# Batch 2's first dense layer by seven half-size products

## The chip, the cores and the metric

The kernel runs on one core of a Trainium2 chip. The metric is the device time of one execution in microseconds. PE below is the tensor engine (PEld its weight loads, which overlap its products), DVE the vector engine, ACT the scalar engine, POOL the GpSimd engine, SP the engine that only issues transfers here.

## The reference

Attention with a sliding window and sink tokens, and behind it a dense layer, a squared ReLU and a second dense layer:

```python
# q, k, v: (4 batches, 8 heads, 768 tokens, 64), float32; n_sink = 4, window = 128
scores = q @ k.T / sqrt(64)
keep   = (key < 4) | (0 <= query - key < 128)
a      = softmax(where(keep, scores, -1e9))
x      = (a @ v), heads side by side           # (3072 tokens, 512)
h      = x @ w_in                              # w_in  (512, 2048)
g      = maximum(h, 0) ** 2
out    = g @ w_out                             # w_out (2048, 512), float32
```

## The kernel before

The kernel works in bf16 with float32 sums. It takes one batch of 768 tokens after another, in three steps of 256 tokens (`s`), and lays the attention of batch b+1 between the dense layers of batch b, so that PE always has something to multiply. Every piece of work is an operation of a small planner (`op(...)`), with the engines it may run on and what it comes after. Which operation is issued when, on which engine, and in which room of a pool, isn't decided at run time: the string `ORDER` lists the operations by number, with a letter where the engine was chosen (d, a, g for DVE, ACT, POOL) and a `+0` or `+1` for the pool. Each engine then works through its list strictly in that order, and waits where an input or a room isn't ready.

**Attention.** K and Q of batches 2 and 3 are loaded by POOL (lines 393, 403 for V) and turned by transposing transfers on SP's queue (line 449). PE makes scores (line 602), ACT the exponentials (623), POOL or DVE the masks (213, 632, 635), PE the values (671), DVE the division (687, 688), and SP's queue turns the result into `xT` (702).

**First dense layer, plain form** (`layer1`, line 752): for 2 or 4 blocks of 128 hidden features, four products each over the 512 inputs, with 512 or 256 tokens as the moving columns, into a PSUM room of pool `den`. Then a ReLU (DVE 765 or ACT 763) and a square (DVE 774 or ACT 772) into `gT_sb`. Batches 0, 1 and 2 use it.

**First dense layer, fast form** (`layer1_fast` and `quad`, line 872): batch 3 alone uses it (`FAST = (3,)`). It halves the hidden features, the inputs and the tokens, and makes the 2 by 2 block product with seven half-size products instead of eight (Strassen). A quad is one group of blocks: seven products of 8 matmuls with 128 tokens, or of 4 matmuls with 256 tokens. It holds two PSUM banks from its first product to its last reading, in pool `den` or `att`; `den` and `att` have two rooms each, and `att` also serves the scores and the values. Around the products stand sums of tokens (line 830; for a single step of 256 tokens after a spreading copy `xd` on ACT), a copy of the first product (ACT or DVE, 187/189), two subtractions (DVE, 913), a ReLU for half of the result (ACT 928 or DVE 930), a sum with saturation for the other half (DVE, 940), and two squares (894, 896). Inside a quad these alternate with the products: the fifth product waits for the copy, the fourth and third for the subtractions, the sixth and seventh for the ReLU.

**Weight sums.** The fast form needs five sums of weight blocks of `w_in`. Each was one DVE operation of 2048 elements a partition (line 796). Three were written over `qkT_all[0]` (free once batch 2's attention is done), two into rooms of pool `qr`, which has five.

**Second dense layer**: the plain form for two thirds of batch 0 (961), and the same seven-product scheme (`layer2_fast`, line 1071) elsewhere, with its sums (1029), additions out of PSUM (1096, 1112, 1119) and copies.

Of the kernel before, what the change touches and what calls it, by code (L numbers as in the profile page):

```python
# [21 lines left out]
0 8 7 9 1 5 10 11 2 12 13 3 14 15 55d 57+0 16 19 59a 20 17 56d 21 18 61d 63+0 22 58 62d 65a 60d 64 6 67a 83+1 79 66a  # L22
68d 69+1 85 70 71d 103+0 84+0 105 73g 74d 72d 23 75+1 86 76 77d 91+0 78a 24 87+1 93 25 89 88 92+0 80 26 114+1 90 94
95+0 4 96 117 97 106g 99+1 98 104+0 107 100d 101 118g 81+1 102d 113+0 108d 156 115 127 82 116d 119+1 157a 121 27 28
120 109+0 111 29 30 31 32 33 158a 122 162 110 112 123+1 125 168 126a 124d 163d 171 169d 164d 165 172a 173d 159 166a
167a 128 131 130d 129d 177 160a 133a 132a 137 145 140 174 148 161d 178d 179d 136 144 289 290 146 149d 170d 147d 138
139d 134 141d 135 175d 34 208g 291 35 36 37 38 39 40 41 42 43 44 45 46 47 48 49 50 51 52 53 54 355 356 292 150 142
143 151 293 294 274 295 152 154 153d 296 297a 176a 298a 155d 186 275 187a 276 277 196+0 180 198a 183 181a 182a 184a
197 204+1 205 199d 188d 200+0 201 192+0 193 189 206a 207d 194d 203d 195d 190d 202a 219+0+0 191d 185d 357 358 359 220
222 278 279 212+0+1 213 215 300 209 301 280 281 373 385d 223 302 237+0+0 210+1 282 299 374 375 376 211 238 240 304  # L30
305 214 239d 306d 230+0+0 307 308 233 231 216 303 311 309d 310 217+0 221 224+0 312 315 234g 232g 313 218 360 314 225
235+0 283 316 241d 242+0 236 317a 284 243 361 362 363 364 365 366 367 368 369 370 371 226+1 228 251+0 229d 286a 227a
244+0 246 252d 253d 245a 285 247d 389 287d 248+1 390 392 340 249d 250d 256+0+0 341a 325 259 257 391 260d 393 326d
386 254+0 322 258g 382 255 342a 263+0+0 323a 261+1 334 262 324d 335d 264 266 265g 396 383 379 288 378 372 267d 331
397 399 398 327a 337 268+0 332d 377 380 384 381 269 319 338a 339d 270+0 271a 272 320d 400 273a 336a 333a 328 321d
329d 330d 456 394 401 352 343 437 353a 349 344a 402 395 530 560g 531 532 533 551 534 535 536 537 538 539 458 318 405
350a 457 351d 441 443d 439 438 345d 406 408 346 412 442 444 445 415 553 403 347d 413 447 409g 416g 428 348a 446a 549
554 548 407g 429 440 448 449 450 414d 451 460 387 354a 461 452 431 388 410 417 475 476 453 454a 479 411 432g 430g
480 463 481a 459 477 418 478 421 482 483 550 552 455 419 422 484a 424 555 404 465a 423g 425g 420 462a 485 433 486
487 490 464 434 488 426 672 489 466 427 467 468 471 580 540 541 542 543 544 545 491 492d 469 494 581 583 470 472  # L40
473d 503 670 495d 435 493 556 559 436 558 557 496a 564 500 565 567 504d 669 509 501d 566 587 510a 512 505a 588 590
568 561 673 511d 497 513d 571 515 574 671 498d 499a 569 572 506 502d 570 514d 516a 575 573 603 521 606 604 507d 522d
546 584g 591g 605g 547 527 576 562 577 518 517a 508a 528a 612 613 582d 631 632 633 519a 563 520a 589g 524 596 597
# [68 lines left out]
def kernel(  # L112
# [11 lines left out]
    nc = tc.nc  # L124
# [245 lines left out]
    def load_v(b, s, behind=None, yields=()):  # L370
# [8 lines left out]
        ops["cast", b, s] = o  # L379

    def load_natural(b, s, older_values):

        begun = [ops["layer1", b - 2, 0, 0], w_out_op[3]]
        for ti in (1, 0):
            if s == 0:
# [395 lines left out]
    def weight_sums_in(key, after):  # L781
# [4 lines left out]
        for n, (name, x, y, how) in enumerate(((1, A[0][0], A[1][1], ALU.add), (2, A[1][0], A[1][1], ALU.add),  # L786
# [4 lines left out]
            def run(e, n=n, name=name, x=x, y=y, how=how, slot=slot):  # L791
                if slot is None:
                    wi_sb[name] = spare[n]
                else:
                    wi_sb[name] = bank(slot, "wi", [128, 2, 2, 512], BF16)
# [473 lines left out]
```

## Time and profile before

| | |
|---|---|
| median of 3 runs | 213.5 us (213.03 to 213.55) |
| the profiled execution | 213.66 us, its span 211.9 us |
| PE busy | 204.0 us, 96% of the span |
| DVE busy | 167.8 us, 79%, 303 instructions |
| ACT busy | 112.9 us, 53%, 146 instructions |
| POOL busy | 97.9 us, 46% |
| granted PE clock | 1.00 |
| weight loads (PEld) busy | 165.1 us, 78% |

The 1.76 us between the profiled execution's time and its span lie before the first and after the last instruction. The mean duration of an instruction is longer than its distance to the next one: on PE the ends are modelled and overlap, and on DVE and ACT the groups add up to about 181 and 120 us, against 167.8 and 112.9 us busy, because one instruction begins before the one ahead has quite ended. So PE work is counted here by the pieces of the chain (start to start), and sums on DVE and ACT are scaled by 167.8/181 = 0.93 and 112.9/120 = 0.94.

### The profile page before, as it was taken

The numbers are of one execution on the slowest core, as the hardware profiler recorded it, in microseconds if no ns is written. First come the engines' busy times: TensorE is split into PE (matmuls) and PEld (weight loads), VectorE is DVE, ScalarE is ACT, GpSimd is POOL, SyncE is SP. The second block draws the span as 40 slices with busy tenths as digits, with TensorE's granted clock in tenths as the row PEclk, the third lists the DMA queues.
The fourth block names the chain that finished last, engine by engine and source line by source line (L and its number), as shares of the span: only waits on it lengthen the run. The fifth ranks groups of instructions, "written<-read, shape, count | busy, mean of one in ns | idle before, by whom it ended". The sixth has DMA issues, their size and how long they took to land.

```text
span 211.9 us, 5455 instructions
## 1 busy us (share of the span) xinstructions
PE 204.0 (96%) x2282; PEld 165.1 (78%) x2287; DVE 167.8 (79%) x303; ACT 112.9 (53%) x146; POOL 97.9 (46%) x139
## 2 busy tenths in 40 slices
PE   3999999999999999999999999999999999999993
PEld 3858997579569645589888964569899999998892
DVE  7487747795898847798776699997979989899963
ACT  2497277249652488567854234887931017976100
POOL 7989696598409965792851951216400000000000
PEclk9999999999999999999999999999999999999999
DMA  5999999999992999999933899304404504000205
GB/s 138 295 186 206 174 198 215 161 155 143 146 186 34 131 148 158 160 152 155 190 74 128 105 119 200 79 0 46 130 0 53 152 0 172 29 2 3 86 16 200
DMA packets 93625, 26.09 MB, mean 123 GB/s; under 512 B 86816, under 2 KB 91552, under 8 KB 93600
## 3 DMA queue, kind: packets, MB, share of 16 engines
q0 software_dynamic: 69248, 12.59, 83.1%
q1 hardware_dynamic: 24168, 13.07, 25.4%
q8 instruction: 18, 0.29, 0.6%
q10 hardware_dynamic: 184, 0.07, 0.1%
q14 instruction: 7, 0.06, 0.1%
HBM read 27.30 MB, written 6.29 MB: 159 GB/s over the span
## 4 chain that ended last, share of the span: by engine, by line
PE 95%; DVE 2%; POOL 1%; issue 1%; ACT 0%; DVEq 0%; POOLq 0%
PE pm L752 30%; PE py L1071 28%; PE pm L872 9%; PE po L671 7%; PE py L961 7%; PE ps L602 6%; PE pt L495 3%; PE pt L180 2%; PE px L720 1%; PE pk L561 1%; PE ps L595 1%; PE ya L1071 0%; DVE kblk L537 0%; DVE xn_sb L688 0%; POOL sg L213 0%
## 5 line engine op out<-in xcount | busy, mean ns | idle before, releaser
L752 PE MATMUL pm<-xT,w_in_sb 128*128 128x256 bf16 (+1 forms) x448 | 66.8, 304 | 0.0
L752 PEld LDWEIGHTS <-w_in_sb 128*128 128x128 bf16 x448 | 48.0, 114 | 12.6 <-issue 1.6
L623 ACT ACTIVATE expm<-ps 128x1024 bf16<-128x1024 f32 (+1 forms) x48 | 43.8, 952 | 17.7 <-PE ps L602 17.6
L213 POOL TENSOR_SCALAR_AFFINE_SELECT expm<-expm 128x512 bf16<-128x512 bf16 x38 | 26.6, 729 | 45.7 <-ACT expm L623 32.6
L1071 PEld LDWEIGHTS <-gT_sb 128*128 128x128 bf16 x336 | 31.0, 98 | 4.0 <-issue 0.7
L765 DVE TENSOR_SCALAR r<-pm 128x1024 bf16<-128x1024 f32 x19 | 23.2, 1221 | 3.3 <-PE pm L752 3.3
L1071 PEld LDWEIGHTS <-sg 128*128 128x128 bf16 x240 | 22.9, 98 | 3.2 <-issue 0.5
L763 ACT ACTIVATE r<-pm 128x1024 bf16<-128x1024 f32 x17 | 17.4, 1021 | 14.8 <-PE pm L752 14.8
L1071 PE MATMUL py<-wt,sg 128*128 128x256 bf16 x160 | 20.8, 273 | 0.0
L1071 PE MATMUL py<-wt,gT_sb 128*128 128x256 bf16 x160 | 20.6, 273 | 0.0
L772 ACT ACTIVATE gT_sb<-r 128x1024 bf16<-128x1024 bf16 x18 | 18.9, 1061 | 2.0 <-DVE r L765 1.9
L187 ACT ACTIVATE osb<-py 128x256 f32<-128x256 f32 (+1 forms) x15 | 6.4, 427 | 23.3 <-PE py L1071 7.9
L1071 PE MATMUL py<-w_out_sb,gT_sb 128*128 128x256 bf16 x144 | 18.7, 273 | 0.0
L688 DVE TENSOR_TENSOR xn_sb<-po,rc 128x512 bf16<-128x512 f32 (+1 forms) x28 | 17.2, 615 | 1.0
L671 PEld LDWEIGHTS <-expm 128*128 128x128 bf16 x352 | 16.3, 97 | 2.1 <-issue 0.5
L671 PE MATMUL po<-v,expm 128*128 128x65 bf16 x352 | 17.3, 193 | 0.1
L774 DVE TENSOR_TENSOR gT_sb<-r 128x1024 bf16<-128x1024 bf16 x18 | 13.6, 761 | 1.9 <-ACT r L763 1.8
L961 PE MATMUL py<-w_out_sb,gT_sb 128*128 128x512 bf16 x59 | 14.7, 380 | 0.4 <-issue 0.2
L602 PE MATMUL ps<-qkT 64*128 64x128 bf16 (+1 forms) x256 | 14.4, 238 | 0.0
L602 PEld LDWEIGHTS <-qkT 64*128 64x128 bf16 x256 | 8.1, 94 | 8.0 <-issue 6.3
L671 PE MATMUL po<-vs,es 128*128 128x65 bf16 x128 | 12.8, 193 | 0.0
L687 DVE RECIPROCAL rc<-po 128x8 f32<-128x8 f32 (+1 forms) x28 | 5.5, 196 | 8.4 <-PE po L671 8.3
(100 smaller groups left out, 336.5 us busy)
## 6 DMA issues: line engine op xcount, KB each, us to landing
out_dram<-osb SPq DMA_DIRECT2D x11, 512.0 KB, 3.3
v<-in_v_dram POOLq DMA_DIRECT2D x24, 128.0 KB, 6.9
qn<-in_k_dram POOLq DMA_DIRECT2D x20, 128.0 KB, 6.3
qn<-in_q_dram POOLq DMA_DIRECT2D x20, 128.0 KB, 6.4
w_in_sb<-in_moe_w_in_dram POOLq DMA_DIRECT2D x4, 512.0 KB, 9.3
w_out_sb<-in_moe_w_out_dram POOLq DMA_DIRECT2D x4, 512.0 KB, 9.2
qr<-in_k_dram SPq DMA_DIRECT2D x4, 256.0 KB, 5.3
qr<-in_q_dram SPq DMA_DIRECT2D x4, 256.0 KB, 5.0
```

The lines of the kernel that those rows point to most:

```text
L213: nc.gpsimd.affine_select(out=e_tile, in_=e_tile, compare_op=ALU.is_ge, fill=fill, base=i - 1, pattern=[[0, n], [1 if i else -1, 128]], ch ...
L602: nc.tensor.matmul(ps[:, h2, o:o + w], lhsT=qkT_sb[r, m, 1, c, :], rhs=qkT_sb[r, m, 0, qb:qb + w // 128, :], start=(i == 0 and not biased) ...
L623: nc.scalar.activation(out=x[:, :, o:512], in_=bank_t["s", b, s, m][:, :, o:512], func=AF.Exp, scale=scale)
L671: touch(("po", b, s, m0), e, nc.tensor.matmul(pv[:, i, h2, :], lhsT=lhsT, rhs=rhs, start=(n_ == 0), stop=(n_ == len(mms) - 1)), j)
L688: touch(("po", b, s, m0), e, nc.vector.tensor_tensor(out=xn_sb[:, 2 * s:2 * s + 2, 128 * (m0 + j0):128 * (m0 + j0 + nj)].rearrange("p i (j ...
L752: nc.tensor.matmul(pm[:, i, :], lhsT=w_in_sb[:, fb // 4, kb, fb % 4:512:4], rhs=xT[:, c0 // 256:(c0 + cw) // 256, kb, :], start=(kb == 0), ...
L763: nc.scalar.activation(out=o, in_=h, func=AF.Relu)
L765: nc.vector.tensor_scalar_max(o, h, 0.0)
L772: nc.scalar.activation(out=g, in_=r, func=AF.Square)
L872: touch(tag, e, nc.tensor.matmul(y[:, bk, i, :], lhsT=weights(name, f0 + i, a), rhs=rhs[:, a, :], start=fresh and i == 0 and a == 0, stop= ...
L961: touch((b, u), e, nc.tensor.matmul(pm[:, i, :], lhsT=gT_sb[:, fb, 128 * t:128 * t + 128], rhs=w_out_sb[:, fb, :], start=(fb == 0), stop=( ...
L1071: ins = nc.tensor.matmul(y_, lhsT=x[:, i, :], rhs=r_, start=(first or tail and n == 2) and i == 0, stop=i == HB - 1, skip_group_check=not ...
```

## The change

Batch 2 too takes the fast form of the first dense layer (`FAST = (2, 3)`). The five sums of weights are therefore made one batch earlier, during batch 1's first dense layer, and each in two halves of 1024 elements. Products 1, 6 and 7 get two rooms of `qr`, held from then on. Sums 2 and 5 are written in place over the blocks of `w_in` that no plain product and no other sum needs any more; they come after the last plain product of batch 1. Batch 3's loads come after the first of the sums, since these take two of the five rooms in which K and Q arrive. Two smaller edits: token sums of 256 columns come from pool `qs` rather than `expm`, and K and Q of batches 2 and 3 lose one ordering condition in `attention` (which no operation of these two batches used). The whole list `ORDER` is new, from the first words to the last; it moves many operations between engines and places.

```diff
-    NAMES = (1, 2, 5, 6, 7)
-    wi_sb, wi_slot = {}, {}
-
-    def weight_sums_in(key, after):
+    wi_sb = {}
+
+    def weight_sums_in(key, last):
...
-        spare = qkT_all[0].rearrange("p (n i a f) -> n p i a f", n=3, i=2, a=2)
-        for n, (name, x, y, how) in enumerate(((1, A[0][0], A[1][1], ALU.add), (2, A[1][0], A[1][1], ALU.add),
-                                               (5, A[0][0], A[0][1], ALU.add), (6, A[1][0], A[0][0], ALU.subtract),
-                                               (7, A[0][1], A[1][1], ALU.subtract))):
...
-                nc.vector.tensor_tensor(out=wi_sb[name], in0=x, in1=y, op=how)
-            ops["wi", name] = op(key + 0.01 * n, {"dve": 1.26}, run, after=after, takes=[slot] if slot else [])
+        slots = [Slot("qr", 99), Slot("qr", 99)]
+        spec = ((1, A[0][0], A[1][1], ALU.add, (0, 0), (0, 1)), (6, A[1][0], A[0][0], ALU.subtract, (0, 2), (1, 0)),
+                (7, A[0][1], A[1][1], ALU.subtract, (1, 1), (1, 2)))
+        for n, (name, x, y, how, *places) in enumerate(spec):
+            for a, (d, j) in enumerate(places):
...
+                    nc.vector.tensor_tensor(out=tiles[d][:, j], in0=x[:, :, a], in1=y[:, :, a], op=how)
...
+        for name, x, y, old in ((2, A[1][0], A[1][1], 6), (5, A[0][1], A[0][0], 7)):
+            for a in range(2):
+                def run(e, name=name, x=x, y=y, a=a):
+                    wi_sb[name, a] = x[:, :, a]
+                    nc.vector.tensor_tensor(out=x[:, :, a], in0=x[:, :, a], in1=y[:, :, a], op=ALU.add)
+                ops["wi", name, a] = op(key + 0.03 + 0.004 * a, {"dve": 0.7}, run, after=[ops["wi", old, a]] + last)
...
                 o.after += begun
+                if b - 1 in FAST:
+                    o.after += [ops["wi", 1, 0]]
...
-            pool = "qs" if len(names) == 1 else "expm"
+            pool = "qs" if len(names) * hw <= 256 else "expm"
...
-    NATURAL, TURNED, BIASED, FAST = (2, 3), (), 1, (3,)
+    NATURAL, TURNED, BIASED, FAST = (2, 3), (), 1, (2, 3)
...
-            weight_sums_in(b - 0.1, [ops[x] for x in ops if x[0] in ("scores", "sinks") and x[1] == 2])
...
+        if b + 1 == FAST[0]:
+            weight_sums_in(b + 0.4, [ops[x] for x in ops if x[0] == "layer1" and x[1] == b])
```

## The prediction

> **What bounds the kernel now.** I read the page's busy line first, then the chain of waits, the list of who waited for whom, the chain in order of time, and last the busy time by stretches.
>
> ```profile
> PE 204.0 (96%) x2282; PEld 165.1 (78%) x2287; DVE 167.8 (79%) x303; ACT 112.9 (53%) x146; POOL 97.9 (46%) x139
> ```
> ```profile
> PE 95%; DVE 2%; POOL 1%; issue 1%; ACT 0%; DVEq 0%; POOLq 0%
> ```
> ```profile
> PE px L720 <- DVE xn_sb L688: 0.3, 1, 0.3
> ```
>
> The chain that ends last is PE work for 95% of the span. Among PE's waits, after the 3.5 us at the start, the largest is 0.3 us. So from 3.5 us on PE is handed work without a gap, and a PE matmul less is time less, as long as the other engines keep up. The chain in order of time gives the price of both forms of the layer. The pieces below are batch 2's plain form (line 752; 16 and 8 matmuls are of 512 columns, 32 of 256) and batch 3's fast form (line 872; 32 of 128 columns, and 144, of which 112 are of 256 columns).
>
> ```profile
> 128.88 3.58 PE pm L752 x16
> ...
> 137.02 1.85 PE pm L752 x8
> ...
> 139.24 1.73 PE pm L752 x8
> ...
> 145.83 3.62 PE pm L752 x32
> ...
> 164.38 1.79 PE pm L872 x32
> ...
> 175.81 14.04 PE pm L872 x144
> ```
>
> The busy time by stretches (length, then PE, PEld, DVE, ACT, POOL, clock, DMA) shows who else is near full:
>
> ```profile
> 130.00:140.00 10.00, 10.00 (x73) 5.27 (x72) 9.70 (x14) 6.58 (x8) 1.92 (x2) 1.00 0.49 108
> 140.00:150.00 10.00, 10.00 (x110) 8.56 (x109) 8.46 (x14) 8.11 (x10) 3.30 (x5) 1.00 0.39 72
> 176.00:190.00 14.00, 14.00 (x144) 13.95 (x142) 13.27 (x19) 10.99 (x14) 0.00 (x0) 1.00 0.20 77
> ```
>
> From 130 to 150 (batch 2's plain layer beside batch 3's attention) DVE has 0.9 of its time taken, 97% from 130 to 140; from 176 to 190 (batch 3's quads, with no attention beside them) it is 13.27 of 14, 94.8%, and PE still has no gap. The change brings these two together.
>
> **PE work.** Removed: 64 matmuls of 512 columns and 64 of 256. The eight in 1.73 us give 0.216 us each, and 32 of 256 columns in a gapless stream 3.49 us, 0.109 each: 13.84 + 6.98 = 20.8 us. The chain's own pieces for these 128 add up to 21.56, since a piece ahead of scores or values is 0.12 us longer; that hand-over stays where the new products also alternate with scores and values. Added: the 224 matmuls that batch 3 already runs; its chain pieces add up to 0.45 + 0.45 + 1.79 + 0.45 + 1.34 + 14.04 = 18.5 us. So PE loses 2.3 us, or 3.0 if no hand-over comes back. I take 2.4.
>
> Here a rule stands against the change. The row first: 32 matmuls of 128 columns in 1.79 us are 0.056 us each, so half as many columns cost half as much. The Trainium skill's page "TensorE: Matmul & The Clock Gate", section "Back-to-back issue gap", puts a sustained stream of weight loads and matmuls of 128 columns near 81 ns a matmul, which would make small products poor value: an estimate by that page is 2.8 us more for batch 2's 112 matmuls of 128 columns, and no saving. The sum goes by the trace's 56 ns.
>
> **DVE work.** From the built kernel's order and the rows of before. Added for batch 2's quads: 12 subtractions (L913, 0.683 each: 8.2), 6 saturated sums (L940, 1.217: 7.3), which take the place of 7 ReLUs that DVE did (1.221: -8.5), 8 token sums (0.284 x 3, 0.418, 0.42 x 3, 0.686: 3.2) and 2 copies of a first product (0.69: 1.4). The weight sums: five of 1.22 (6.1) become ten halves, costed at 0.69 by the other operations of 1024 bf16 elements (6.9). Small moves to and from ACT and POOL: -3.2. Together 9.2 us of durations, 8.5 after the overlap factor of 0.93. ACT gains 8.3 durations, 7.7 net: ten squares of the new form less nine of the old (1.06), one ReLU (1.02), four copies of 0.595 (2.4), the spreading copy (1.05), six copies taken over from DVE (3.6), less 0.8 of other copies. POOL gains two mask operations (1.5).
>
> Where this lies: the six halves for products 1, 6, 7 and three of the four in-place sums stand in batch 1's first dense layer and behind it. There DVE's list holds 34.5 us against 39.5 us of PE; they are costed at nothing, hidden by that PE work. If the cover were gone, they would cost at most 9 x 0.65 = 5.9 us. The sums that leave batch 3's neighbourhood give nothing, since PE had no gap there.
>
> The critical stage is the one from batch 2's first product to its last. I counted each engine's list in it. PE: 18.5 for the products, 40 second-layer matmuls (4.4), scores (0.44 + 0.55 + 0.44), values (2 x 0.36) and sink scores 0.33: 25.4 us. DVE: twelve subtractions, five saturated sums, four masks of 0.551, five token sums, two normalisations of 0.9, six operations of 1024 elements, one in-place sum and three smaller ones: 27.2 us of durations, 25.3 after overlap. ACT: 23.7, of which 5.9 are exponentials for batch 3. So in this stage DVE has as much to do as PE, ACT almost as much, and they depend on each other at every product. Bounds for the PE gaps that follow: 0 if DVE never idles; 25.3 / 0.948 = 26.7 us of stage, 1.3 us of gaps, if DVE can only be as dense as in the last stretch above, the nearest row. Part of that lag can be carried into the second layer behind, where DVE's list is again below PE's. I take 0.9 us. A gain from gaps is excluded: PE can't do the stage in less than its matmuls.
>
> The likeliest places: the sixth product of the second quad, which waits for that quad's ReLU on ACT; ahead of it in ACT's list stand two exponentials of 1.02 for batch 3. And the second products of the 512-token quads, which need DVE to free a PSUM room by the saturated sum (1.22).
>
> **Waits that are added.** Batch 3's K and Q reuse batch 2's rooms, so POOL's load waits for all of batch 2's turns; behind it on POOL stand the other loads, V, the sink values and a mask. Between that load and the first scores of batch 3 about 37 us of PE work stand in the order, and a load (6.4 us to land) with eight turns (1.2 each) and the last one's landing (3.4) takes 19.4: nothing. The last two tiles are closer. Their four loads stand on POOL between masks, SP turns them one after another, and the sink scores and the last scores of batch 3 wait for them. The longest landing of a turn was 5.7 instead of 3.4: 0 to 2.3 us, taken at 0, by the median. The in-place sums wait for PE's last plain product of batch 1, long past by then. The rest of the new `ORDER` (batches 0 and 1) has the same PE matmuls, and DVE at 65 to 90% of PE's time except in one stretch, the last plain products of batch 0 with three weight sums of `w_out` and the first masks of batch 1: 14.3 us of DVE beside 13.5 of PE. If DVE has nothing done ahead, PE waits 0.8 there; at best its 0.3 of before goes. I take 0.3.
>
> **Sum.** -2.4 + 0.9 + 0.3 = -1.2 us: the profiled execution would go from 213.66 to 212.5. The median of the runs shown is 0.16 below it, so I give 212.3.
>
> **The rivals.**
>
> *Everything is hidden.* PE stays gapless as it did at 94.8% DVE; then 213.5 - 2.4 = 211.1, or 210.5 at the 3.0. For it: PE's waits of before are nearly nil with DVE at 97% from 130 to 140. Against: that stretch had no chain from product to product. 0.20.
>
> *DVE and ACT take it back.* The stage gets its 1.3 us of gaps, and another 1.1 come from late turns and batch 0: no change, 213.5 within 0.6. 0.16.
>
> *ACT's list sets the pace of the quads.* Place: the six ReLUs of batch 2's quads on ACT, each with an exponential (1.02) or a square (1.06) of another piece ahead, while the sixth and seventh products wait and the four PSUM rooms are full, so that PE has nothing else queued. Price: up to 1.0 us a quad; with four of the six hit, 4.1 us, so 213.5 - 2.4 + 4.1 = 215.2. It decides from 0.40 us a quad (2.4 / 6). For it: ACT's 23.7 of 25.4 us, and that PE takes its list strictly in order. Against: in 176 to 190 the same ReLUs at 11.0 of 14 us made no gap. 0.18.
>
> That the change doesn't do what it says is excluded: the built kernel has 64 fewer matmuls of 512 columns, 64 fewer of 256 at line 752, and 224 more in the quads.
>
> **How the numbers follow.** My case (gaps of 0.6 to 1.7 us, 211.7 to 212.8) has 0.46. About 0.3% (0.64 us) is what a measurement of this kernel tells from no change. Faster by more: 0.46 + 0.20 = 0.66; within: 0.16; slower: 0.18. The range of 210.9 to 213.9 takes in the first rival at 2.4 and the bounds of my case; it leaves out some 0.05 below and 0.15 above.
>
> **What would show it.** In the changed profile: line 752's matmuls of 512 columns (now 757) down to 64, and about 37 us for the 448 quad matmuls (now 887); DVE above 90% and ACT near 90% in batch 2's quads; PE waits of 0.3 to 0.8 us on ACT's ReLU or DVE's saturated sum there, about 1 us together. Wrong if PE waits on transfers, if gaps in batches 0 and 1 exceed 0.8 us, if batch 2's quads run with no gap at all, or if PE's gaps exceed 2.4 us.

## The result, and the profile after

The changed kernel takes 214.51 us (median of 8 runs, 214.14 to 215.49), the kernel before beside it 213.53 us (8 runs, 212.52 to 213.69). The ratio is 1.0062, with a 95% interval of 1.004 to 1.0084. So the change makes the kernel slower by about 0.6%; the forecast was 212.3 us, and faster. The profiled execution of after took 214.40 us (213.66 before), its span 212.7 us (211.9).

First the busy time of each engine, and the chain that ended last by engine, in the page of after:

```profile
PE 202.3 (95%) x2378; PEld 169.4 (80%) x2383; DVE 177.7 (84%) x322; ACT 120.8 (57%) x158; POOL 104.0 (49%) x141
```
```profile
PE 83%; DVE 8%; ACT 4%; issue 2%; POOL 1%; DVEq 0%; POOLq 0%; ACTq 0%
```

The arithmetic was saved: PE has 1.7 us less busy time. But the chain is now PE for 83% of the span instead of 95%, with DVE and ACT holding 12%. The list of waits after (engine, line, releaser, then total, times and longest in us) names them. In before nothing behind the start exceeded 0.3 us.

```profile
PE po L676 <- ACT expm L628: 0.7, 1, 0.7
PE pm L887 <- ACT r L943: 0.7, 1, 0.7
PE py L1086 <- DVE sg L1044: 0.5, 2, 0.3
PE pm L887 <- ACT expm L628: 0.2, 1, 0.2
```

Three of the four stand close together, as the timeline of PE shows (start, duration, line, work; in brackets the idle time ahead and its releaser):

```profile
130.68 0.61 PE L887 MATMUL pm<-xs,w_in_sb 128*128 128x128 bf16 x8
131.22 0.50 PE L607 MATMUL ps<-qkT 64*128 64x256 bf16 x8
132.41 1.05 PE L887 MATMUL pm<-xs,wi 128*128 128x128 bf16 x16 [0.68 <-ACT r L943]
134.21 0.52 PE L676 MATMUL po<-v,expm 128*128 128x65 bf16 x12 [0.75 <-ACT expm L628]
...
135.85 1.03 PE L887 MATMUL pm<-xs,wi 128*128 128x256 bf16 x8 [0.25 <-ACT expm L628]
```

The first line is the third product of batch 2's second quad, the second batch 3's scores, the third the sixth and seventh products of that quad. The latter wait for the quad's ReLU (1.03 us on ACT, 131.33 to 132.36), and only 0.44 us of scores stand in between. The other two wait for exponentials. A releaser in this list is only the last link. The chain in order of time, from 130 on, shows what stands ahead of it:

```profile
130.17 0.74 DVE xs L845 x2
130.91 1.13 issue
132.04 1.22 DVE r L955
...
133.34 0.81 ACT expm L628
134.15 0.95 ACT gT_sb L909
135.10 0.71 ACT expm L628
...
135.85 1.25 PE pm L887 x10
```

The exponential at 133.34 is late because the saturated sum of the first quad (DVE, 132.04) frees the `expm` room it writes to. That sum is late because something of 1.13 us, which the chain can only call "issue", stands after the token sums on DVE. The timelines of DVE and POOL show what it is:

```profile
130.17 1.95 DVE L845 TENSOR_TENSOR xs<-xT 128x512 bf16<-128x512 bf16 x2
132.04 1.21 DVE L955 CUSTOM_DVE_ANT_1 r<-pm,t 128x1024 bf16<-128x1024 f32 x1
133.17 0.41 DVE L845 TENSOR_TENSOR xs<-xT 128x512 bf16<-128x512 bf16 x1
133.50 0.68 DVE L911 TENSOR_TENSOR gT_sb<-r 128x1024 bf16<-128x1024 bf16 x1
134.19 0.90 DVE L637 TENSOR_TENSOR expm<-expm,mask 128x768 bf16<-128x768 bf16 x1
```
```profile
130.57 1.26 POOL L215 TENSOR_SCALAR_AFFINE_SELECT expm<-expm 128x512 bf16<-128x512 bf16 x2
131.74 1.80 POOL L396 DMA_DIRECT2D qn<-in_q_dram  x2
133.52 2.06 POOL L215 TENSOR_SCALAR_AFFINE_SELECT expm<-expm 128x512 bf16<-128x512 bf16 x2
```

A token sum of the same size takes 0.41 us at 133.17. The second of the pair at 130.17 takes 1.61 us, while POOL runs two masks in a row. The mask of DVE at 134.19 takes 0.90 us instead of 0.55 while POOL is masking again. Together that is 1.54 us of DVE, in a stretch where DVE has no room for it. The busy time by stretches (length, then PE, PEld, DVE, ACT, POOL, clock, DMA), first of after, then of before:

```profile
126.00:140.00 14.00, 12.33 (x184) 11.46 (x183) 13.69 (x22) 11.52 (x15) 11.30 (x14) 1.00 1.37 132
140.00:149.00 9.00, 9.00 (x84) 8.35 (x82) 8.26 (x13) 7.35 (x8) 0.00 (x0) 1.00 0.29 39
```
```profile
126.00:140.00 14.00, 14.00 (x97) 7.25 (x96) 12.96 (x17) 9.26 (x11) 3.14 (x4) 1.00 1.04 110
```

From 126 to 140 DVE is busy 13.69 of 14 us while PE, full in before, does 12.33. Behind it DVE still has 92% of its time taken: there is little to catch up with.

At the very end the order of the last stores on SP changed too (timeline of SP, first of before, then of after; line 1160 is 1175 after, 1141 is 1156, 1157 is 1172):

```profile
207.41 0.33 SPq L1160 DMA_DIRECT2D out_dram<-osb  x1
208.28 0.33 SPq L1141 DMA_DIRECT2D out_dram<-osb  x1
```
```profile
208.57 0.34 SPq L1156 DMA_DIRECT2D out_dram<-osb  x1
208.97 0.42 SPq L1175 DMA_DIRECT2D out_dram<-osb  x1
209.45 0.92 SPq L1172 DMA_DIRECT2D out_dram<-osb  x2
```

Before, the store of the last quarter (1160) went out while another was still being computed. After, it stands behind the first quarter's, and the two last stores begin 0.88 us behind that one. PE's last products, meanwhile, start at 206.58 instead of 206.30, 0.28 us later.

**The account, start to start.** PE's quad work saves 2.3 us (20.8 to 18.5). The waits add 2.6, each stretch taken as after less before: 2.1 from 120 to 140 (the three waits there are 0.84, 0.91 and 0.41 when the pitch of the matmul ahead is subtracted from the distance of starts, which counts a little more than the idle time in the list), 0.8 from 140 to 170 (the largest wait 0.45 at 156.2), 0.5 from 50 to 62, and -0.8 in the first 20 us, where the first loads land. That last part belongs to this pair of profiles: the 200th matmul starts anywhere from 18.8 to 20.4 us in the profiles of this case. The end adds 0.5. -2.3 + 2.6 + 0.5 = 0.8, the difference of the spans.

### The profile page after: what moved, and what is told of

The parts are those of the page before. It is cut to its first block, busy times and chain, and to the rows that moved or that the text cites. A ratio compares the mean times of both kernels' runs of the same rounds, so it can differ in the third digit from the quotient of the medians.

```text
span 212.7 us, 5708 instructions
## 1 busy us (share of the span) xinstructions
PE 202.3 (95%) x2378; PEld 169.4 (80%) x2383; DVE 177.7 (84%) x322; ACT 120.8 (57%) x158; POOL 104.0 (49%) x141
## 3 DMA queue, kind: packets, MB, share of 16 engines
q0 software_dynamic: 69248, 12.59, 81.2%
## 4 chain that ended last, share of the span: by engine, by line
PE 83%; DVE 8%; ACT 4%; issue 2%; POOL 1%; DVEq 0%; POOLq 0%; ACTq 0%
PE py L1086 26%; PE pm L757 19%; PE pm L887 15%; PE po L676 7%; PE py L976 5%; PE ps L607 4%; PE pt L182 2%; PE pt L500 2%; ACT gT_sb L909 1%; PE px L725 1%; DVE sg L1044 1%; ACT expm L628 1%; DVE gT_sb L779 1%; DVE qkT L191 1%; DVE t L928 1%
## 5 line engine op out<-in xcount | busy, mean ns | idle before, releaser
L215 POOL TENSOR_SCALAR_AFFINE_SELECT expm<-expm 128x512 bf16<-128x512 bf16 x40 | 31.0, 807 | 40.1 <-ACT expm L628 37.5
L757 PE MATMUL pm<-xT,w_in_sb 128*128 128x256 bf16 (+1 forms) x320 | 44.7, 294 | 0.0
L757 PEld LDWEIGHTS <-w_in_sb 128*128 128x128 bf16 x320 | 34.1, 114 | 6.2 <-issue 0.8
L887 PEld LDWEIGHTS <-w_in_sb 128*128 128x128 bf16 x256 | 21.7, 114 | 0.5 <-issue 0.3
L887 PE MATMUL pm<-xs,wi 128*128 128x128 bf16 (+1 forms) x192 | 19.8, 246 | 0.9 <-ACT r L943 0.7
L770 DVE TENSOR_SCALAR r<-pm 128x1024 bf16<-128x1024 f32 x12 | 14.7, 1222 | 6.1 <-PE pm L757 6.0
L676 PE MATMUL po<-v,expm 128*128 128x65 bf16 x352 | 17.9, 193 | 0.9 <-ACT expm L628 0.7
L887 PEld LDWEIGHTS <-wi 128*128 128x128 bf16 x192 | 16.4, 114 | 1.6 <-issue 1.4
L928 DVE TENSOR_TENSOR t<-t,pm 128x512 f32<-128x512 f32 x24 | 16.0, 683 | 1.5 <-PE pm L887 1.2
L768 ACT ACTIVATE r<-pm 128x1024 bf16<-128x1024 f32 x12 | 12.3, 1026 | 7.2 <-PE pm L757 7.1
L955 DVE CUSTOM_DVE_ANT_1 r<-pm,t 128x1024 bf16<-128x1024 f32 x12 | 14.5, 1218 | 0.8 <-PE pm L887 0.8
```

The source lines that it names most:

```text
L215: nc.gpsimd.affine_select(out=e_tile, in_=e_tile, compare_op=ALU.is_ge, fill=fill, base=i - 1, pattern=[[0, n], [1 if i else -1, 128]], ch ...
L676: touch(("po", b, s, m0), e, nc.tensor.matmul(pv[:, i, h2, :], lhsT=lhsT, rhs=rhs, start=(n_ == 0), stop=(n_ == len(mms) - 1)), j)
L757: nc.tensor.matmul(pm[:, i, :], lhsT=w_in_sb[:, fb // 4, kb, fb % 4:512:4], rhs=xT[:, c0 // 256:(c0 + cw) // 256, kb, :], start=(kb == 0), ...
L770: nc.vector.tensor_scalar_max(o, h, 0.0)
L887: touch(tag, e, nc.tensor.matmul(y[:, bk, i, :], lhsT=weights(name, f0 + i, a), rhs=rhs[:, a, :], start=fresh and i == 0 and a == 0, stop= ...
L928: touch(tag, e, nc.vector.tensor_tensor(out=T["t"], in0=T["t"], in1=T["y"][:, bk], op=ALU.subtract), bk)
```

## The experiments

All kernels are the changed kernel with the edit shown, unless said otherwise; numbers in `ORDER` are operations. "PE idle" is 30 us less PE's busy time from 120 to 150; it is 0.00 in before and 1.68 in after, and repeats within 0.03 where the order there is the same (e1_tail, e9_act_squares_out). "DVE busy" is of the same stretch (26.31 in before), and repeats only within 0.6. Each median is compared with runs of the kernel before beside it (213.12 to 213.38; 213.53 for after).

| run | median, us | ratio to before, 95% interval | PE idle | DVE busy |
|---|---|---|---|---|
| after | 214.51 | 1.0062, 1.004 to 1.0084 | 1.68 | 28.38 |
| e1_tail | 214.12 | 1.0039, 1.0017 to 1.006 | 1.67 | 27.80 |
| e2_masks_later | 214.26 | 1.0042, 1.0022 to 1.0061 | 1.22 | 27.74 |
| e3_masks_out | 215.83 | 1.0105, 1.0084 to 1.0126 | 3.13 | 26.53 |
| e4_cover | 214.43 | 1.0049, 1.0027 to 1.0072 | 1.51 | 27.86 |
| e7_edits | 213.97 | 1.0037, 1.0022 to 1.0051 | 1.21 | 27.72 |
| e8_dve_masks_out | 213.55 | 1.0021, 1.0006 to 1.0035 | 0.79 | 26.37 |
| e9_act_squares_out | 214.80 | 1.0075, 1.0055 to 1.0095 | 1.65 | 27.78 |
| e10_edits_copies | 219.01 | 1.027, 1.0251 to 1.0289 | 3.07 | 24.68 |
| e11_moves | 214.44 | 1.0039, 1.0021 to 1.0058 | 1.61 | 27.08 |
| e12_moves_pe | 216.06 | 1.0121, 1.0076 to 1.0166 | 3.09 | 24.89 |
| e13_before_fewer | 211.86 | 0.9927, 0.9901 to 0.9954 | 0.57 | 27.14 |
| e14_rooms | 214.42 | 1.0066, 1.0048 to 1.0084 | 1.59 | 27.77 |
| e15_rooms_edits | 213.66 | 1.0034, 1.0018 to 1.0051 | 1.21 | 27.71 |
| e16_rooms_cover | 214.24 | 1.0055, 1.0036 to 1.0074 | 1.76 | 27.19 |
| e17_rooms_cover_copy | 214.32 | 1.0053, 1.0033 to 1.0072 | 1.79 | 26.67 |
| e18_saturated_first | 213.99 | 1.0021, 1.0005 to 1.0037 | 1.20 | 27.56 |
| e19_saturated_cover | 214.42 | 1.0057, 1.0035 to 1.008 | 1.59 | 27.24 |
| e20_saturated_cover_copy | 214.29 | 1.0053, 1.0033 to 1.0074 | 1.61 | 26.52 |

### Theory and rivals

Theory: DVE's own list is too dense from 126 to 140, made denser by POOL's masks, and the products hang on it. Rivals: the ReLU's latency alone (too little PE work as a cover); ACT's list, as in the prediction; the pool rooms; the tail.

### The tail: e1_tail

```diff
-881 883 882 884 886 885
+881 886 883 882 884 885
```

Operation 886 is the last quarter's store, 885 the last one.

> One word of ORDER moved: the store of the last quarter (line 1174) is issued as soon as its sum is done, ahead of the two stores of the first quarter, as in the kernel before. Theory A (the new ORDER lost the tail: in the changed profile the final pair of stores is issued 0.78 us later than before, and only 0.29 us of that is PE's): 214.5 - 0.5 = 214.0, the last SP issue about 0.5 us earlier. Theory B (the last transfers are bound by their landing, not by when they are issued): 214.5, no change.

The last quarter's store goes out first again, and the two issues that begin last come 0.40 us behind the first quarter's instead of 0.88 (timeline of SP in this run):

```profile
207.99 0.34 SPq L1175 DMA_DIRECT2D out_dram<-osb  x1
208.87 0.34 SPq L1156 DMA_DIRECT2D out_dram<-osb  x1
209.27 0.90 SPq L1172 DMA_DIRECT2D out_dram<-osb  x2
```

So about 0.5 us of the loss is the order of the stores. The ratio goes from 1.0062 to 1.0039, the same 0.5 us, though the intervals overlap; PE's idle time in the quads is unchanged.

### POOL's masks away from DVE's sums: e2_masks_later

```diff
-656g 611 612 658g 613 614
+611 612 613 614 656g 658g
```

656g and 658g are masks of batch 3's second step on POOL, 611 to 614 the loads for the last tiles.

> Two masks on POOL (lines 215, for batch 3's step 1) moved behind four loads in POOL's list. Theory A (POOL's masks and DVE's sums of two SBUF operands exclude each other: the sum at 130.5 took 1.61 us instead of 0.42, and this delay of 1.2 us is what PE waits for at 134.2 and 135.9): that sum takes 0.42 again, the saturated sum behind it starts at about 130.9 instead of 132.0, the waits of PE at 134 and 136 (0.91 and 0.41) go, and the time is 214.5 - 1.2 = 213.3. Theory B (DVE's and ACT's lists are full here, as the prediction had it): the waits stay, 214.5 within 0.3.

The timeline of DVE in this run:

```profile
130.38 0.76 DVE L845 TENSOR_TENSOR xs<-xT 128x512 bf16<-128x512 bf16 x2
131.19 1.22 DVE L955 CUSTOM_DVE_ANT_1 r<-pm,t 128x1024 bf16<-128x1024 f32 x1
...
132.67 1.12 DVE L911 TENSOR_TENSOR gT_sb<-r 128x1024 bf16<-128x1024 bf16 x1
133.71 0.98 DVE L637 TENSOR_TENSOR expm<-expm,mask 128x768 bf16<-128x768 bf16 x1
```

The two token sums take 0.76 us instead of 1.95, and the saturated sum follows at once. PE's wait at 134.2 (0.91 us) is gone, the one at 135.9 falls from 0.41 to 0.28, and PE's idle time falls by 0.46. The rest comes back: the moved masks now meet DVE's mask at 133.71 (0.98 instead of 0.55) and another at 136.59 (0.78), and 0.42 and 0.33 us of waits on the saturated sum and a subtraction appear further on. Moving a collision inside a full stretch wins part of it.

### DVE masks taken out: e8_dve_masks_out

The edit of e2_masks_later, and in the mask's operation:

```diff
+                            if b == 3 and s == 0:
+                                return
```

> On top of the two POOL masks moved, DVE's four masks of batch 3's step 0 (line 637, 0.55 us each, 2.2 us in all between 127 and 138) are left out. Theory A (DVE's list sets the pace of batch 2's quads): the waits of PE at 135 to 139 (0.28, 0.42, 0.33) go, and the ReLU's wait at 132.6 (0.84) shrinks or stays, as it hangs on PE's order: 214.3 - 1.0 = 213.3. Theory B (the chain from product to product, with its latencies, sets the pace whatever DVE has to do): the waits only move, 214.3 within 0.3.

With 1.4 us less DVE work than in e2_masks_later (26.37 against 27.74), PE's idle time falls by another 0.43, to 0.79. The list of PE's waits, the start's left out, is down to the ReLU and small ones:

```profile
PE pm L889 <- ACT r L945: 0.7, 1, 0.7
PE py L1088 <- DVE sg L1046: 0.5, 2, 0.3
```

In e2_masks_later PE waited for none of these masks, only for the saturated sum and a subtraction that stood in the same list, so what gave the 0.43 here is a shorter list on DVE, not a mask that PE waited for. Of the 1.68 us, 0.46 go with the place of POOL's masks and 0.43 with DVE's own list. (DVE's busy time didn't fall measurably at the first step: 27.74 in e2_masks_later against 27.80 in e1_tail. What changed there is where POOL's masks hold it up.) 0.68 is the ReLU, which neither touched, and 0.1 is left.

### ACT's list lightened: e9_act_squares_out

```diff
             def run(e):
+                if b == 2 and len(ss) == 1 and e == "act":
+                    return
                 x = T[r]
```

> Against the changed kernel: ACT's three squares of batch 2's first two quads (line 909, 1.06 us each) are left out. The prediction's rival (ACT's list sets the pace of the quads): all three waits at 132 to 136 shrink, 214.5 - 1.5 = 213.0. Theory A (DVE's list and one ReLU latency): the waits at 132.4 (0.84) and 134.2 (0.91) stay, since ACT was free ahead of both; only the one at 135.9 (0.41) goes, as the exponential it waits for stands behind one of these squares: 214.5 - 0.4 = 214.1.

ACT's busy time from 120 to 150 fell from 22.40 to 19.28 us, but PE's first two waits are the same, and there is a third again (timeline of PE, shifted by 0.47 us by the start):

```profile
132.88 1.05 PE L887 MATMUL pm<-xs,wi 128*128 128x128 bf16 x16 [0.68 <-ACT r L945]
134.68 0.52 PE L676 MATMUL po<-v,expm 128*128 128x65 bf16 x12 [0.74 <-ACT expm L628]
...
136.75 0.49 PE L887 MATMUL pm<-xs,wi 128*128 128x256 bf16 x3 [0.23 <-DVE r L957]
```

The third wait of after, for an exponential that stood behind one of these squares, is gone. In its place PE waits at the next product, for DVE's second saturated sum. So ACT's list didn't set the pace, though ACT is named as releaser: ACT itself was late because of DVE's room, or, at the ReLU, because PE came too early.

### Masks of the next step out: e3_masks_out

```diff
+                            if b == 3 and s == 1 and m0 == 2:
+                                return
```

> The same two masks left out altogether (four operations of POOL; two heads pairs of batch 3's step 1 stay unmasked). Theory A (exclusion of DVE by POOL): as with the masks moved, 213.3, or up to 0.3 less if the moved masks only collide with another DVE operation (the mask on DVE at 134.2 took 0.90 instead of 0.55). Theory B (full lists): 214.5, since neither DVE's nor ACT's list gets shorter.

The edit left out more than the expectation says: all four masks of that step, eight POOL instructions (40 to 32). POOL then issued its loads 10 us earlier, and this moved the turned K and Q: two waits for a turn appear in PE's list, and PE's idle time nearly doubles.

```profile
PE ps L607 <- DMA qkT<-qn: 2.3, 2, 1.2
```

The wait at 134.2 is gone, as it is in e2_masks_later, but the time says nothing on the masks. The run is inconclusive on its question; what it shows is that the turns of batch 3 have no slack against POOL's order.

### Cover for the ReLU: e4_cover

```diff
-513 515 533 534 514 538 539 655 657 535 537 536d 516 638
+513 515 514 538 539 655 657 516 533 534 535 537 536d 638
```

516 is the second quad's third product, 533 and 534 are the first quad's sixth and seventh, 535 its saturated sum. The two products now stand behind 516, between it and the wait for the ReLU.

> PE's order in the first two quads of batch 2: the sixth and seventh product of the first quad moved behind the third product of the second, so that they and the scores (0.9 + 0.44 us) stand between that product and the sixth one of the second quad. Theory A (the wait of 0.84 us at 132.4 is the latency of one ReLU, 1.03 us, with only 0.44 us of scores to cover it; ACT was free when the third product ended): the wait at 132.4 goes, 0.3 of it comes back as a wait for the second subtraction ahead of the third product; the later waits at 134 and 136 stay as they hang on DVE: 214.5 - 0.5 = 214.0, or no gain if they take it all. Theory B (ACT's list, two exponentials ahead of that ReLU, sets the pace): the wait stays at 0.7 to 0.9.

The wait for the ReLU shrinks from 0.84 to 0.16 us, so the cover was the cause there. But product 516 now comes so early that it waits 0.52 us for its subtraction on DVE, and the wait behind grows from 0.91 to 1.07. In all PE's idle time falls by 0.17 us: the wait for the ReLU can be moved, and most of it comes back as waits that hang on DVE.

### More orders: e7_edits, e10_edits_copies, e11_moves, e12_moves_pe

e7_edits has the edits of e1_tail and e2_masks_later, second-layer sum 717 three places later, and a weight sum of `w_out` (276), in the dense stretch at 58 us, behind operation 302:

```diff
-717 692 698 699
+692 698 699 717
```

> Four edits of ORDER together, the computation unchanged: the tail's store early, the two POOL masks behind the four loads, batch 2's sums for its second token pair (line 1044) ahead of the one for its third, and the third weight sum of w_out (line 1017) behind the two sums that PE waits for at 58.4. Theory A (part of the loss is where the new ORDER puts single operations): 0.5 from the tail, 0.4 from the masks as measured, 0.45 from the sums (the wait at 156 goes), 0 to 0.4 from the weight sum: 214.5 - 1.5 = 213.0, 0.2 below the kernel before. Theory B (DVE, 97% busy from 100 to 140, gives each gain back as another wait): 214.0, that is the tail alone.

The wait at 156.2 is gone, and that at 58 us came back as 0.53 at 64.6 us. The ratio is 1.0037 instead of 1.0062, PE's idle time that of e2_masks_later.

e10_edits_copies adds three copies of batch 1's output moved from DVE to ACT (`456d 475d 502d` to `a`):

> The four edits of ORDER and three copies of 256 columns (0.42 us each on DVE, between 106 and 124) given to ACT, which is 34% busy from 110 to 120. Theory A (DVE's list is the bound from 100 to 140, so time taken off it is time): DVE 1.26 us less, the waits at 133 to 139 shrink by another 0.5 to 1.0: 213.0 - 0.7 = 212.3. Theory B (latency): as with the four edits alone, 213.0 to 214.0.

Three copies fewer on DVE, and 5.0 us more than e7_edits: on ACT the copies stand behind exponentials, and the first products of batch 2 wait for one of them (list of PE's waits).

```profile
PE pm L887 <- ACT osb L189: 2.1, 1, 2.1
PE py L1086 <- DVE osb L1111: 1.6, 1, 1.6
```

e11_moves has the tail, the masks and 717 of e7_edits, moves a copy of a first product to ACT (`511d` to `511a`), a mask (633) ahead of a subtraction, and two token sums (538, 539) 20 places later:

> ORDER edited where the traces showed a price, the computation unchanged: the tail's store early, the two POOL masks behind the loads, the two sums of line 1044 swapped; and new: the copy of the second quad's first product (0.68 us on DVE) given to ACT, which is idle there, one mask ahead of the subtraction that waits for it, and two token sums (0.42 each) that are needed only at 138 taken from ahead of the saturated sum at 131 and put behind it. Theory A (in batch 2's quads the order and length of DVE's list sets the pace): PE's waits at 135.3, 136.2 and 139.5 (0.28, 0.42, 0.32) go, the ReLU's latency of 0.84 at 132.6 stays: 213.7 - 0.7 = 213.0, ratio to before 0.998 to 1.0. Theory B (every place that DVE leaves is taken by the next latency): 213.7, ratio 1.003.

DVE has 0.6 us less than in e7_edits from 120 to 150, but PE's idle time is 1.61, 0.4 more. The sum of DVE's work isn't all that counts: the moved copy and mask changed which operation is late, and waits of 0.56 and 0.32 us stand further on. e12_moves_pe adds the order of products of e4_cover (533 left in place) and a later place for values 636:

> The same, and PE's order changed at the ReLU: the seventh product of the first quad behind the third product of the second one, so that 0.9 instead of 0.44 us of PE work cover that ReLU, and the first two products of the next quad ahead of batch 3's values. Theory A (0.84 us at 132.6 is one ReLU's latency of 1.03 us less its cover): the wait falls to about 0.3, another 0.5 us: 212.5, ratio to before 0.996. Theory B (the saturated sum that frees the PSUM room, now 0.45 later, is the limit): the wait moves to the next quad's first product, no gain over the run without it.

Here PE waits 2.58 us for an exponential right behind 636, and the time goes to 216.06. This is a fault of the edit and no verdict on the cover.

### The PE work alone: e13_before_fewer

The kernel before, with one of four products left out for the first block of each of batch 2's operations (8 matmuls of 512 columns and 4 of 256):

```diff
-                for kb in range(NKB):
+                nk = NKB - (b == 2 and i == 0)
+                for kb in range(nk):
```

> The kernel before with 8 matmuls of 512 and 4 of 256 columns of batch 2's plain first layer left out (the fourth product of the first block of each operation), 8 x 0.216 + 4 x 0.109 = 2.16 us of PE work, with the work of all other engines as it was. Theory A (a PE matmul less is time less as long as nothing is added elsewhere, the prediction's first term): 213.3 - 2.1 = 211.2, ratio 0.990. Theory B (DVE, 9.7 of 10 us busy from 130 to 140, already sets the pace there): 212.0 or more, ratio above 0.994, with new waits of PE for DVE between 130 and 145.

By the pitches 2.16 us of PE work are gone, and nothing is added on any engine. The time falls by 1.56 us (1.0 to 2.1 by the interval). Behind the first 20 us the list of PE's waits has two new ones, on the engines that make the ReLU:

```profile
PE pm L753 <- ACT r L764: 0.3, 1, 0.3
...
PE pm L753 <- DVE r L766: 0.2, 1, 0.2
```

DVE is busy 9.92 of 10 us from 130 to 140 in this run, and PE idles 0.57 us from 120 to 150, where it had no idle time in before. So even free of charge, PE's saving in this place pays about 0.7 of its size (0.5 to 1.0 by the interval): DVE's 9.70 of 10 in before, which looked like a hidden engine, was within 0.3 us of being the bound.

### A ninth room: e14_rooms to e17_rooms_cover_copy

The pool `expm` gets nine rooms instead of eight, so that the exponential need not wait for the saturated sum:

```diff
-    sizes = dict(att=2, den=2, qr=5, qs=6, expm=8, r=3, osb=2, sg=4, u=2)
+    sizes = dict(att=2, den=2, qr=5, qs=6, expm=9, r=3, osb=2, sg=4, u=2)
```

> The changed kernel with nine instead of eight rooms in pool expm, nothing else. The exponential that PE's values wait for at 134.2 then takes a room that a product of PE freed long before, instead of the one that the saturated sum frees at 133.3. Theory A (the waits at 134.2 and 135.9 hang on this room, not on how much DVE or ACT have to do): that exponential starts right behind the ReLU, at about 132.4 instead of 133.3, the wait of 0.91 goes and the one of 0.41 goes or shrinks: 214.5 - 1.1 = 213.4. Theory B (DVE's list sets the pace): the waits come back at the next products (135 to 140) on line 928 or 955, 214.3.

The wait at 134.2 is gone. PE waits instead for a PSUM room that the second quad's saturated sum frees (DVE, 135.25 to 136.46), the next one in DVE's list (timeline of PE):

```profile
135.06 0.60 PE L887 MATMUL pm<-xs,wi 128*128 128x256 bf16 x4
136.51 0.60 PE L887 MATMUL pm<-xs,wi 128*128 128x256 bf16 x4 [0.85 <-DVE r L955]
```

PE's idle time is 1.59 against 1.68: the room chose the place of the wait, not its size. With the tail, the masks and 717 of e7_edits added (e15_rooms_edits), then the cover (e16_rooms_cover: 534, 535, 537 and 536d behind 516), then `511a` and the earlier mask (e17_rooms_cover_copy):

> Nine rooms, and the three edits of ORDER that paid (the tail's store early, the two POOL masks behind the loads, the two sums of line 1044 swapped). Theory A: 214.5 - 1.1 - 0.5 - 0.45 = 212.5, ratio to before 0.997. Theory B: as the edits without the room, 213.6, ratio 1.002.

> As the run with rooms and edits, and the seventh product of the first quad behind the third product of the second, so that 0.9 us of PE work stand between that product and the sixth one. Theory A (the wait of 0.84 at 132.6 is the ReLU's latency less its cover): it falls to 0.3: 212.0, ratio 0.995. Theory B (the second subtraction is late, DVE sets the pace): 0.4 of it comes back ahead of the third product or behind the seventh: no gain over the run without it.

> As the run before, and the copy of the second quad's first product on ACT instead of DVE (0.68 us), with a mask of DVE drawn ahead. Theory A: another 0 to 0.3 if the second subtraction was late, 211.8. Theory B: no difference, or 0.3 worse as ACT's list gets longer.

e15_rooms_edits measures what e7_edits did, in time (1.0034) and idle time (1.21). The cover lowers the ReLU's wait to 0.61 us, and a wait of 1.43 us on the saturated sum comes (e16_rooms_cover). Less DVE work on top changes nothing (1.79). The timeline of DVE in e17_rooms_cover_copy shows why:

```profile
130.18 0.69 DVE L928 TENSOR_TENSOR t<-t,pm 128x512 f32<-128x512 f32 x1 [0.63 <-PE pm L887]
...
132.12 1.23 DVE L955 CUSTOM_DVE_ANT_1 r<-pm,t 128x1024 bf16<-128x1024 f32 x1 [0.58 <-PE pm L887]
```

DVE now waits for PE: the first quad's saturated sum stands until the seventh product, which was moved back as cover, is done, and everything behind it in DVE's list is late with it. DVE is busy only 12.59 of 14 us from 126 to 140 here, and PE idles all the same.

### Saturated sums first: e18_saturated_first to e20_saturated_cover_copy

On e15_rooms_edits, the second quad's saturated sum (521) is placed ahead of a mask, and an exponential ahead of a square:

```diff
-641 519 520 518a 642 636 521 569+0 570 639 571a
+641 519 520 639 518a 521 642 636 569+0 570 571a
```

> As the run with nine rooms and three edits, and two operations swapped: the saturated sum of batch 2's second quad ahead of one of batch 3's masks on DVE, and on ACT one exponential ahead of a square. Theory A (PE's wait behind the ReLU's is the time until DVE reaches the saturated sum that frees a PSUM room): the sum starts at about 133.9 instead of 135.2, the waits at 135 to 140 (0.22, 0.48, 0.32) fall to 0.2 to 0.4 together, the ReLU's 0.84 stays: 213.7 - 0.7 = 213.0, ratio to before 0.999. Theory B (DVE has too much to do from 126 to 140, whatever comes first): the sum of the waits stays within 0.2 of 1.9.

The waits at 135 and 136 us are gone, and PE's values now wait for a mask of DVE (136.77 to 137.50, 0.73 us instead of 0.55; timeline of PE):

```profile
137.55 0.54 PE L676 MATMUL po<-v,expm 128*128 128x65 bf16 x12 [0.30 <-DVE expm L637]
...
139.34 0.93 PE L887 MATMUL pm<-xs,w_in_sb 128*128 128x256 bf16 x7 [0.16 <-DVE t L928]
```

PE's idle time is 1.20, as in e2_masks_later. Its ratio of 1.0021 is the lowest of all the reorderings, and still not faster than before. The two that add the cover, and the cover and `511a`:

> The same with the seventh product of the first quad behind the third product of the second, as cover for the ReLU. Theory A (with DVE's order mended, the ReLU's latency is what is left): the wait of 0.84 falls to 0.6 as in the run with rooms and cover, and does not come back behind it: 212.8. Theory B: the saturated sums, now later, take it back: as without the cover, 213.0, or 0.5 worse.

> The same with the copy of the second quad's first product on ACT (0.68 us less on DVE ahead of the second subtraction) and one mask drawn ahead. Theory A (DVE's length): another 0.2 to 0.4, 212.5, ratio 0.997. Theory B (order, not length): as the run before.

Both are back at 1.6 us of idle time.

### What the runs tell together

Twelve orders of the same work (e1, e2, e4, e7, e11, and e14 to e20) have 1.2 to 1.8 us of idle PE from 120 to 150. What lowered it was to keep POOL's masks off DVE's operations (-0.46) and to take DVE work out (-0.43). Taking ACT work out left it as it was, and a room moved it. So in the changed kernel's order DVE is the bound of that stretch, in part by its amount, in part through POOL. Its amount isn't all: in e17_rooms_cover_copy and e20_saturated_cover_copy DVE has 12.59 and 12.33 of 14 us, and PE still idles 1.79 and 1.61. There DVE and PE wait for each other in turn, since each keeps strictly to its list. It stays open how the remaining 0.7 us at the ReLU splits between its latency and DVE's pace, since every order that covered the ReLU put a DVE operation late. No version with all of the work beat the kernel before.

## Why the prediction was wrong

**PE work, -2.4 us: right in size, wrong as a gain.** The trace has -2.3, and the small products ran at the price that the sum took: 16 of 128 columns in 0.89 us, 0.056 each. But the sum took it as time, one for one, and e13_before_fewer shows 1.56 of 2.16 where nothing else changes. The prediction named the condition ("as long as the other engines keep up"), and read 97% DVE from 130 to 140 beside a full PE as a sign for it. It is the opposite: 0.3 us of slack in 10, and a PE that is 2 us faster needs more.

**Gaps in batch 2's quads, +0.9 us, bounds 0 to 1.3: the step that failed.** The trace has 2.1 us from 120 to 140, in the quads and above the upper bound, and 0.8 from there to 170 (0.45 of it at 156.2, in the second layer behind, where the prediction expected to catch up): 2.9 in all. That is also above the 2.4 us that the prediction itself gave as a sign of being wrong. It went wrong three times.
1. DVE's list was held against PE's over the whole stage (25.3 of 25.4 us). The stage isn't even: DVE has 13.69 of 14 us from 126 to 140, with batch 3's masks and batch 2's token sums, and 8.26 of 9 behind.
2. The 94.8% row was used as an upper bound of the loss. A row in which nobody waits bounds nothing from above: it shows a density that was reached with chains of one kind, and here two kinds crossed.
3. Durations came from rows of operations that mostly ran with POOL idle. POOL's masks in the new order overlap them, at 1.54 us in the decisive stretch.

The first two are argued from the rows, and explain why bounds of 0 to 1.3 could be left behind; the third is measured by e2_masks_later, which won 0.46 of it. POOL may have a part in the wait at 156.2 too: the two sums ahead of it ran beside masks and took 1.07 and 0.78 us instead of 0.68. e7_edits took that wait away by the order of the sums, so POOL's share there isn't shown.

**The likeliest places: right, the reason for the first wrong.** PE did wait at the sixth product of the second quad for its ReLU, 0.7 us in the list. The two exponentials stood ahead, but ended at 131.28, as the third product did (131.29): they held nothing up. It was PE's cover that was short: 0.44 us of scores beside 1.03 us of ReLU (e4_cover took that wait down to 0.16). Where the product comes earlier, the two exponentials do hold the ReLU up, by 0.2 us (e16_rooms_cover: product done at 131.28, ReLU at 131.51). The second place, the PSUM room that the saturated sum frees, shows in e14_rooms at 0.85 us, at the first product of a 512-token quad, which takes the room, and not at the second as the prediction has it. In after it hardly shows, because the first quad's saturated sum was late for an `expm` room before that.

**Rest of `ORDER`, +0.3 us: about right.** From 50 to 62 us 0.5 were added, where DVE's weight sums of `w_out` stand, as named. The -0.8 at the start is variation.

**Transfers, nothing: right for the changed kernel.** PE has no wait for a transfer in after. e3_masks_out shows how near it was: with POOL's loads 10 us earlier, 2.3 us of waits for turns.

**The end of the kernel, not in the sum: missed.** 0.5 us came from the order of three stores on SP. SP's list of the built kernel had shown it; the prediction didn't cost it.

**DVE work, +8.5, and ACT, +7.7:** measured +9.9 and +7.9. The prediction put nothing for DVE operations that POOL holds up. Added up over the traces, DVE's operations on two SBUF inputs were longer than usual by 5.8 us in after and 2.1 in before, 1.54 of it in the decisive stretch. That is more than the 1.4 us by which DVE's work exceeds the sum, so the rest of that list came out lower than costed.

**The rivals.** "Everything is hidden" fails on the waits. "DVE and ACT take it back" has the right mechanism with a price of 2.4 us that was still too small. "ACT's list sets the pace" ended on the right side for a wrong reason: e9_act_squares_out took 3.1 us off ACT, and nothing moved.

Put right, with the sum's own terms: -2.3 + 2.9 + 0.5 + 0.5 = +1.6 us for the profiled execution, less 0.8 that the start gave. The medians, over which the start varies for both kernels, differ by 1.0. The ratio of 1.0062 is 1.3 us of 213.53, 0.9 to 1.8 by its interval, which takes in the 1.6.

## What to carry to other kernels

Before giving work to an engine at 97% of a stretch, count its list over the few microseconds in which the new chain is densest, not over the stage, and treat a row without waits as slack to be measured, not as a bound. A product-to-ReLU-to-product chain needs other PE work between them, here about 1.3 us for a ReLU of 1.03 (0.44 of scores and a wait of 0.84), and each room, sum and mask that it hangs on has to be early. Moving POOL work costs nothing on POOL's account, but look at which DVE operation it will lie beside, and at the last stores of the program.

## What the runs showed of the hardware

**DVE's operations on two SBUF inputs are held up beside a POOL mask.** Over all 20 profiles (behind the first 20 us), 405 such operations ran beside a POOL mask and nothing else of POOL: 38% of them were longer than usual by over 0.1 us, on average by 0.15, by up to 0.50. With a load's issuing beside the masks too, the most was 0.53 us beside one mask and 1.19 beside two in a row. Of 571 beside POOL's issuing of loads alone the mean is 0.007 us longer, and of 1333 with POOL idle 0.000. The Trainium skill's page "SBUF — State Buffer", section "Who interferes with whom", says that a DVE instruction with two SBUF inputs and a POOL instruction that reads SBUF exclude one another, the first to issue holding the ports. The traces agree: 0.42 us became 1.61 beside two masks, and where DVE was first, POOL's mask took 1.08 to 1.15 instead of 0.63. One thing isn't explained: in e2, e7, e8, e11, e15 and e18 a square of 0.68 us took 1.12 beside the issuing of loads alone.

**The granted clock fell to one half after a wait of PE of over 2 us.** In e10_edits_copies, after a pause of 2.15 us (busy time by stretches):

```profile
128.00:130.00 2.00, 2.00 (x12) 1.44 (x11) 0.00 (x0) 0.60 (x1) 2.00 (x4) 0.50 0.73 281
130.00:132.00 2.00, 2.00 (x25) 1.53 (x24) 0.84 (x2) 0.12 (x1) 2.00 (x4) 0.88 0.99 63
```

The two microseconds after it ran at 0.50. In e12_moves_pe a wait of 2.58 us was followed by 0.50 from 139 to 141. Pauses of up to 1.6 us left it at 1.00 (1.63 in e10_edits_copies itself, at 111.6 us). So in e10_edits_copies the wait took at least another 1.2 us of PE's time: half of the two microseconds at 0.50, and 0.12 of the next two. The Trainium skill's page "TensorE: Matmul & The Clock Gate", section "What's actually happening", has the clock halved after an idle window of about 3.4 us: the half agrees, while the pauses here were shorter.
